# Linear attention and a gated MoE layer on one core: the order in which streamed factors, the next block's x and partial sums are loaded

## The chip, the cores and the metric

The kernel runs on one core of a Trainium2 chip (trn2). The metric is the device time of one execution in microseconds (us); less is better. Loads and stores between DRAM and the core's memory are called transfers or DMAs; all of those named below are issued by SyncE (SP), one after the other, in the order in which they stand in its program.

## The reference

What has to be computed, cut to what matters (8 batches, 8 heads, 576 positions, head size 64, 128 features; the second half has 4608 tokens, a model width of 512 and an inner width of 1536):

```python
def phi(x):
    proj = np.einsum('bhsd,df->bhsf', x, w_phi)
    proj = proj - np.max(np.abs(proj), axis=-1, keepdims=True)
    return np.concatenate([np.exp(proj), np.exp(-proj)], axis=-1)
q_p, k_p = (phi(q), phi(k))
kv = np.einsum('bhsf,bhsd->bhfd', k_p, v)
z = np.sum(k_p, axis=2)
num = np.einsum('bhsf,bhfd->bhsd', q_p, kv)
den = np.einsum('bhsf,bhf->bhs', q_p, z)[..., None] + 1e-06
x = (num / den).transpose(0, 2, 1, 3).reshape(4608, 512)
...
a = x @ w_a
b = x @ w_b
out = (a * b) @ w_out
```

## The kernel before

The work has three stages. The attention makes x and writes it to DRAM (`xnorm`, one buffer per batch). The first pass of the MoE layer takes 768 of the 1536 inner columns, in 12 blocks of 384 tokens, and writes its partial result to DRAM (`part`). The second pass takes the other 768 columns, in 6 blocks of T2 = 768 tokens (blocks 0 to 5), adds the partial result and writes `out`. The change is in the second pass, which takes about the last third of the time.

In the second pass the inner columns are three groups, q0, q1 and q2, of 256. For each group a x and b x are computed as a 2 by 2 by 2 block product by a scheme with seven products in place of eight (Strassen and Winograd). Their weight factors have the names of FACTORS (L61), w11, w12, s2, s1, s3, w22 and s4, and they are made ahead of the pass and kept in DRAM (`kept`). x has factors of the same names, made for each block by `factors_of_x` (L655). `winograd` (L702) is the generator that runs the seven products of one group; its `product` (L713) is 12 matmuls at L723 of 128x128 weights by 384 tokens, 6 for a (`pa`) and 6 for b (`pb`). Each number is split into a high and a low part, so each term takes three matmuls. The output products of `second_pass` (L833, `po`) are 126 more matmuls per block, and their weights stay on the core. A block has 21 x 12 + 126 = 378 matmuls.

The 21 factors of a and b don't stay on the core: each is streamed once per block into a tile of 512 KB (`back_s`, `back_w` in the rows; s or w is the first letter of the factor's name). There is a ring of RING = 4 such tiles. Each product ends with `feed()`, which issues the transfer of the next key of the list `order` (L959) into the tile that the product just left:

```python
def feed():
    used[0] += 1
    if used[0] > FIRST and order:
        key = order.popleft()
        fetch(key, ring[0], ...)
```

So the fetch that follows product n brings the weights of the fourth product after it, and waits for the end of product n, which frees the tile. The list goes q by q, each in the order of FACTORS. The products don't: `second_pass` runs the first two products of a group ahead of the last two of the group before it, so the program's order is q0: w11, w12, s2, s1, s3; q1: w11, w12; q0: w22, s4; q1: s2, s1, s3; q2: w11, w12; q1: w22, s4; q2: s2, s1, s3, w22, s4.

Two more kinds of loads stand in the same queue. `factors_of_x` for the next block loads that block's x (L669) into two tiles `x32`, in four transfers (two tiles by two batches; 576 KB and 192 KB, or 384 KB each), all in its first step, at the end of q0; `behind(feeds, ...)` orders each of them behind the fetch issued last. The steps after that split x (casts on ScalarE at L153, differences on VectorE at L160) and form sums of it (L687 to L690 on VectorE). `given_load` (L806 to L812) loads partial sums into tiles `o` of 384 KB, three at the end of q0 and a fourth after the first stores; the results are added to them at L815 (VectorE) and stored from them at L818. The tiles are the ones that the block before stores from.

In a product's wake ScalarE copies a finished pair of PSUM banks (`evict`, L731, into `top0`, `top1` or `low`), and VectorE adds another pair to it (`add`, L735); both free the banks for later products. A scheduler, which simulates the program with a model of time, decides in what order the instructions of each engine stand; the program's order is only its start.

Of the kernel before, what the change touches and what calls it, by code (L numbers as in the profile page):

```python
# [56 lines left out]
FACTORS, AHEAD = ("w11", "w12", "s2", "s1", "s3", "w22", "s4"), 3.2  # L57
# [4 lines left out]
def tile_kernel(ctx, tc, qP, qD, km, kr, vm, vr, w_phi, w_two, eye, w_a, w_b, w_out, out):  # L62
# [13 lines left out]
    nc = tc.nc  # L76
# [8 lines left out]
    NCC = DM // P  # L85
# [71 lines left out]
    def split(hi, lo, src, eng_hi, eng_lo):  # L157

        copy(eng_hi, hi, src)
        eng_lo.tensor_tensor(lo, src, hi, op=ALU.subtract)  # L160
# [228 lines left out]
    def behind(what, issue):  # L389

        with tc.issue_after(what[-1].ins):
            issue()
# [175 lines left out]
    def weight(q, nm, k):  # L568
        key, i = two[q, nm, k]
        return weights[key][:, i]  # L570
# [84 lines left out]
    def factors_of_x(j, pool, xs):  # L655


        n = T2 // 2
        half = NCC // 2
        x = [None] * NCC  # L660
        for c in range(half):
            x32 = pool.tile([P, 2, T2], F32, tag="x32", bufs=2, name=f"x32_1_{j}_{c}")
            x[c], x[c + half] = x32[:, 0], x32[:, 1]
            t = j * T2
            while t < (j + 1) * T2:
                b, s0 = divmod(t, S)
                m, t0 = min(S - s0, (j + 1) * T2 - t), t - j * T2
                rows = xnorm[b].rearrange("(i c p) s -> p c i s", i=2, p=P)[:, c, :, s0 : s0 + m]
                load = lambda: nc.sync.dma_start(x32[:, :, t0 : t0 + m], rows)  # L669
                behind(feeds, load) if j else load()  # L670
                t += m
        yield

        def factor(c, k, src):
            hl = [pool.tile([P, n], F32R, tag=f"x{k}{part}", bufs=half, name=f"x{k}{part}_1_{j}_{c}") for part in "hl"]
            split(*hl, src, nc.scalar, nc.vector)
            xs[c][k] = hl

        for k, i in (("w11", 0), ("w12", half)):
            for c in range(half):  # L680
                factor(c, k, x[c + i][:, :n])
                yield
        for c in range(half):
            (x11, x12), (x21, x22) = ((t[:, :n], t[:, n:]) for t in (x[c], x[c + half]))
            sums = pool.tile([P, 2, n], F32, tag="xs", name=f"xs_1_{j}_{c}")
            t1, t2, t3, t4 = sums[:, 0], sums[:, 1], x12, x21
            nc.vector.tensor_tensor(t1, x12, x11, op=ALU.subtract)  # L687
            nc.vector.tensor_tensor(t2, x22, t1, op=ALU.subtract)
            nc.vector.tensor_tensor(t3, x22, x12, op=ALU.subtract)
            nc.vector.tensor_tensor(t4, x21, t2, op=ALU.subtract)  # L690
            yield
            factor(c, "s2", t2)
            factor(c, "s1", t1)
            yield
            factor(c, "s3", t3)
            factor(c, "w22", t4)
            yield
        for c in range(half):
            factor(c, "s4", x[c + half][:, n:])
            yield  # L700
# [93 lines left out]
    def second_pass(xs, spaces, feed):  # L794
        n = T2 // 2
        pool = pools_moe[-1]
        nq = NFS[1] // 2
        for j in range(NT // T2):
            src, dst = (t.rearrange("(c p) s -> p c s", p=P)[:, :, j * T2 : (j + 1) * T2] for t in (part, out))
            hs = [{} for _ in range(nq)]  # L800
            x_next = factors_of_x(j + 1, spaces["x"], xs) if (j + 1) * T2 < NT else iter(())
            quads = [winograd(q, xs, hs[q], f"1_{j}_{q}", spaces, feed) for q in range(nq)]
            acc, given, us = {}, {}, []

            def at(m, i, t):
                return (slice(None), m + i * (NCC // 2), slice(t * n, (t + 1) * n))  # L806

            def given_load(i, t):
                place = spaces["o"][(0, 1, 2, 0)[2 * i + t]]
                g = place[0].tile([P, 2, n], F32, tag=place[1], name=f"o_1_{j}_{i}{t}")  # L810
                given.update({(m, i, t): g[:, m] for m in range(2)})
                nc.sync.dma_start(g, src[:, i * (NCC // 2) : (i + 1) * (NCC // 2), t * n : (t + 1) * n])  # L812

            def add(key, x):
                nc.vector.tensor_tensor(given[key], x, given[key], op=ALU.add)  # L815

            def store(key):
                nc.sync.dma_start(dst[at(*key)], given[key])  # L818

            def evict(m):  # L820
                nc.scalar.copy(us[0][:, m], acc[m, 0])  # L821
                return us[0][:, m]

            def product(m, k, to, qs):
                start = (m, to) not in acc
                if start:
                    acc[m, to] = pool.tile([P, n], F32, tag="other" if to else "first", bufs=4, name=f"po{to}_1_{j}_{m}")
                for q in qs:
                    w, (hh, hl) = weight(q, "o", k), hs[q][k]
                    cols = slice(m * P, (m + 1) * P)  # L830
                    for n_, (w_, h_) in enumerate(((w[:, 0, cols], hh), (w[:, 0, cols], hl), (w[:, 1, cols], hh))):
                        f = dict(start=(start and q == qs[0] and n_ == 0), stop=(q == nq - 1 and n_ == 2))
                        nc.tensor.matmul(acc[m, to], w_, h_, skip_group_check=True, **f)  # L833

            early, late_, every = range(nq - 1), range(nq - 1, nq), range(nq)
            for q in range(nq):
                for _ in range(3 if q == 0 else 2):
                    next(quads[q])
                    if q == nq - 1:
                        next(x_next, None)  # L840
                        next(x_next, None)
                if q < nq - 1:
                    next(quads[q + 1])
                else:
                    product(0, "w11", 0, early)
                    product(0, "w12", 1, early)
                next(quads[q])
                if q < nq - 1:
                    next(quads[q], None)
                    next(quads[q], None)  # L850
                if q == 0:
                    next(x_next, None)
                    for i, t in ((0, 0), (0, 1), (1, 0)):
                        given_load(i, t)
            product(1, "w11", 0, early)
            product(1, "w12", 1, early)
            product(0, "w11", 0, late_)
            us.append(spaces["brief"].tile([P, 2, n], F32, tag="top0", bufs=2, name=f"u_1_{j}"))
            u = evict(0)
            product(0, "w12", 1, late_)  # L860
            next(quads[-1])
            product(1, "w11", 0, late_)
            u_ = evict(1)
            product(1, "w12", 1, late_)
            next(quads[-1])
            for m, u1 in ((0, u), (1, u_)):
                add((m, 0, 0), u1)
                add((m, 0, 0), acc[m, 1])
                store((m, 0, 0))
            given_load(1, 1)  # L870
            next(x_next, None)
            for m in range(2):
                product(m, "s2", 0, every)
                u2 = evict(m)
                next(x_next, None)
                add((m, 0, 1), u2)
                product(m, "s1", 2, every)
                next(x_next, None)
            for m in range(2):
                product(m, "s3", 0, every)  # L880
                u3 = evict(m)
                next(x_next, None)
                add((m, 1, 1), u3)
                add((m, 1, 1), acc[m, 2])
                store((m, 1, 1))
            for m in range(2):
                product(m, "w22", 0, every)
                add((m, 1, 0), acc[m, 0])
                store((m, 1, 0))
                next(x_next, None)  # L890
                product(m, "s4", 2, every)
                add((m, 0, 1), acc[m, 2])
                store((m, 0, 1))
                next(x_next, None)
            for _ in x_next:
                pass
# [26 lines left out]
    kept, begun, feeds = {}, set(), []  # L923
# [27 lines left out]
    nq = NFS[1] // 2  # L951
# [4 lines left out]
    outs = [(q, "o", k) for q in range(nq) for k in FACTORS]  # L956
    pairs.update({("o", i // 2): outs[i : i + 2] for i in range(0, len(outs), 2)})
    two = {key: (pair, i) for pair, keys in pairs.items() for i, key in enumerate(keys)}
    order = [(q, k) for q in range(nq) for k in FACTORS]  # L959
    own = {key: (first, f"first{i}") for i, key in enumerate(order[:FIRST])}  # L960
    xs = [{} for _ in range(NCC // 2)]
    with ExitStack() as c:
# [29 lines left out]
    order = deque(order * (NT // T2))  # L992
# [81 lines left out]
```

## Time and profile before

| | |
|---|---|
| device time, three runs | 1240.18, 1236.78, 1238.57 us; median 1238.57 us |
| the profiled execution: device time | 1236.89 us |
| the profiled execution: span of the trace | 1235.1 us |
| mean granted TensorE clock, share of full | 0.996 |
| second pass, first matmul to the end of the span | about 815 to 1235 us |
| blocks 1 to 5 of it | one every 69 us or so |

The trace numbers lines as the listing above does. PE is TensorE, PEld its weight loads, DVE VectorE, ACT ScalarE, SP SyncE, which issues the DMAs. A busy share says how much of the time an engine worked; a wait names the instruction that came last of those it waited for. Matmuls overlap: one of 384 columns is shown with 0.335 us, while they start 0.173 us apart, so an idle time of PE between two of them counts from the shown end of the one before. PEclk is the clock granted to TensorE, 1.00 for full speed.

### The profile page before, as it was taken

To read this page: it belongs to the slowest core of one execution; us is meant where nothing else is said; L and a number is where in the kernel's file an instruction comes from. 1 tells how busy PE (TensorE), PEld (TensorE's weight loads), DVE (VectorE), ACT (ScalarE), POOL (GpSimd) and SP (SyncE) were. 2 spreads that over 40 slices of the span, in tenths; PEclk is the share of its full clock that TensorE was granted. 3 is DMA by queue.
4 is the path that set the end of the run, shared out by engine and by line. 5 is a ranking of instruction groups with operands and counts; after the bars stand their busy time and mean duration, and the time that the engine had idled before them with its cause. 6 is when DMAs were issued, how large, how long until landed. Compare 5 with 4: busy or idle time off the path is not lost.

```text
span 1235.1 us, 20179 instructions
## 1 busy us (share of the span) xinstructions
PE 1190.4 (96%) x7086; PEld 1135.3 (92%) x7086; DVE 970.6 (79%) x1733; ACT 782.2 (63%) x1656; POOL 152.4 (12%) x68
## 2 busy tenths in 40 slices
PE   8889999999999999999999999989999999989988
PEld 5467788999999999999999999989999999989988
DVE  7867888988998988898888389968677685957565
ACT  5767778878878887888887446645344352525332
POOL 2322222111222121221221000000000000000000
PEclk9999999999999999999999999999999999999999
DMA  8766774554454454455342588667585858577571
GB/s 233 217 208 178 178 193 121 151 155 121 141 152 141 137 156 124 139 154 150 111 125 71 170 269 291 213 219 238 181 284 175 299 166 294 180 243 227 185 239 64
DMA packets 146165, 225.13 MB, mean 182 GB/s; under 512 B 40912, under 2 KB 87760, under 8 KB 146064
## 3 DMA queue, kind: packets, MB, share of 16 engines
q1 hardware_dynamic: 145616, 223.58, 59.4%
q8 instruction: 56, 0.92, 0.3%
q14 instruction: 45, 0.37, 0.1%
q10 hardware_dynamic: 448, 0.26, 0.1%
HBM read 174.74 MB, written 49.05 MB: 181 GB/s over the span
## 4 chain that ended last, share of the span: by engine, by line
PE 68%; DMA 15%; DVE 10%; ACT 4%; issue 2%; SPq 1%; DVEq 0%; ACTq 0%
PE po L833 10%; PE pa L723 10%; PE pb L723 9%; PE pa L616 8%; PE pb L616 8%; PE po L639 7%; PE kvps L301 6%; PE pn L383 6%; DMA back_s<-kept_s 4%; PE pq L359 2%; DMA raw_b<-in_w_b 2%; PE pk L244 1%; DMA raw_a<-in_w_a 1%; DMA part<-o 1%; DMA k<-in_km 1%
## 5 line engine op out<-in xcount | busy, mean ns | idle before, releaser
L363 POOL PARTITION_ALL_REDUCE mb<-p x64 | 152.2, 2379 | 528.9 <-ACT p L360 430.5
L616 PE MATMUL pa<-xh,w_a 128*128 128x384 f32 x576 | 168.3, 344 | 3.0 <-ACT xh L153 1.8
L616 PE MATMUL pb<-xh,w_b 128*128 128x384 f32 x576 | 163.3, 341 | 0.0
L639 PE MATMUL po<-hh,w_o 128*128 128x384 f32 x576 | 154.3, 340 | 0.1
L616 PEld LDWEIGHTS pa<-xh,w_a 128*128 128x128 f32 x576 | 106.1, 189 | 4.8 <-ACT xh L153 2.1
L616 PEld LDWEIGHTS pb<-xh,w_b 128*128 128x128 f32 x576 | 105.5, 188 | 0.5
L639 PEld LDWEIGHTS po<-hh,w_o 128*128 128x128 f32 x576 | 104.8, 188 | 0.8 <-ACT o L651 0.3
L616 PE MATMUL pa<-xl,w_a 128*128 128x384 f32 x288 | 98.5, 342 | 0.0
L639 PE MATMUL po<-hl,w_o 128*128 128x384 f32 x288 | 97.4, 340 | 0.3 <-DVE hl L160 0.3
L616 PE MATMUL pb<-xl,w_b 128*128 128x384 f32 x288 | 97.5, 339 | 0.0
L160 DVE TENSOR_TENSOR qel<-qe,qeh 128x1152 fp32r<-128x1152 f32 x46 | 62.3, 1355 | 32.4 <-ACT qeh L153 29.6
L833 PE MATMUL po<-hh_s,own_o 128*128 128x384 f32 x288 | 79.9, 335 | 0.3 <-ACT u L821 0.3
L165 DVE TENSOR_TENSOR qs<-q,qs 64x576 fp32r<-64x576 f32 x52 | 64.1, 1233 | 14.5 <-ACT qs L153 12.7
L384 ACT COPY xn<-pn 65x288 f32<-65x288 f32 x128 | 49.1, 395 | 18.3 <-PE pn L383 14.8
L833 PE MATMUL po<-hh_w,own_o 128*128 128x384 f32 x216 | 59.7, 334 | 0.0
L153 ACT CAST qeh<-qe 128x1152 fp32r<-128x1152 f32 x46 | 53.4, 1160 | 2.3 <-PE pn L383 2.3
L639 PEld LDWEIGHTS po<-hl,w_o 128*128 128x128 f32 x288 | 54.1, 188 | 0.7 <-DVE hl L160 0.7
L616 PEld LDWEIGHTS pa<-xl,w_a 128*128 128x128 f32 x288 | 54.2, 188 | 0.3
L367 ACT ACTIVATE qe<-p 128x576 f32<-128x576 f32 x64 | 44.6, 697 | 15.2 <-DVE qel L160 10.2
L616 PEld LDWEIGHTS pb<-xl,w_b 128*128 128x128 f32 x288 | 54.1, 188 | 0.1
L258 ACT ACTIVATE ke<-kd 128x512 f32<-128x512 f32 x64 | 40.8, 637 | 21.1 <-DVE kd L250 18.8
L160 DVE TENSOR_TENSOR kel<-ke,keh 128x1024 fp32r<-128x1024 f32 x42 | 52.4, 1247 | 1.8 <-ACT keh L153 1.6
(301 smaller groups left out, 3431.2 us busy)
## 6 DMA issues: line engine op xcount, KB each, us to landing
back_s<-kept_s SPq DMA_DIRECT2D x71, 512.0 KB
back_w<-kept_w SPq DMA_DIRECT2D x52, 512.0 KB
q<-in_qD SPq DMA_DIRECT2D x52, 288.0 KB
k<-in_km SPq DMA_DIRECT2D x55, 256.0 KB
xun<-xn SPq DMA_DIRECT2D x64, 144.0 KB
x<-xun SPq DMA_DIRECT2D x32, 288.0 KB
rb<-rec SPq DMA_DIRECT2D x32, 288.0 KB
xnorm<-x SPq DMA_DIRECT2D x32, 288.0 KB
```

The source lines that it names most:

```text
L153: eng.copy(dst, src)
L160: eng_lo.tensor_tensor(lo, src, hi, op=ALU.subtract)
L165: eng_lo.tensor_tensor(hi_lo[D:], src[D:], hi_lo[D:], op=ALU.subtract)
L301: nc.tensor.matmul(st["kv_ps", b, pr][:width, j], v_[:, j, :width], e_[:, j], start=(left == NFULL and j == 0 and n_ == 0), stop=(left == ...
L363: nc.gpsimd.partition_all_reduce(mb, p32, P, bass_isa.ReduceOp.absmax)
L367: nc.scalar.activation(e[:, 0], p32, AF.Exp)
L383: nc.tensor.matmul(pn[: D + 1, :HALF], kv_[:, 2 * j + s, :], e_[:, s, tok], **at)
L384: nc.scalar.copy(xn[: D + 1, tok], pn[: D + 1, :HALF])
L616: nc.tensor.matmul(acc, w[:, cc * P : (cc + 1) * P], x, start=(k == 0), stop=(k == 3 * NCC - 1))
L639: nc.tensor.matmul(accs[cc], w[:, cc * P : (cc + 1) * P], h, **at)
L723: nc.tensor.matmul(acc[to][i], w_, x_, skip_group_check=True, **at)
L833: nc.tensor.matmul(acc[m, to], w_, h_, skip_group_check=True, **f)
```

## The change

The list `order` now names the factors in the order in which the program runs the products (FIRST takes its first three keys, and the ring its next four, which are now q0's s1 and s3 and q1's w11 and w12). `factors_of_x` now yields after each of the four x transfers; its first step is taken at the end of q0 as before, two more within q1 and the fourth in q2's turn. The three `given_load` of the end of q0 are now at the end of q1, and every `given_load` is placed behind the fetch issued last. `(nc.sync if j else nc.sync)` is SyncE either way.

```diff
@@ factors_of_x
-                load = lambda: nc.sync.dma_start(x32[:, :, t0 : t0 + m], rows)
+                load = lambda: (nc.sync if j else nc.sync).dma_start(x32[:, :, t0 : t0 + m], rows)
                 behind(feeds, load) if j else load()
                 t += m
-        yield
+                yield
@@ second_pass, given_load
-                nc.sync.dma_start(g, src[:, i * (NCC // 2) : (i + 1) * (NCC // 2), t * n : (t + 1) * n])
+                load = lambda: nc.sync.dma_start(g, src[:, i * (NCC // 2) : (i + 1) * (NCC // 2), t * n : (t + 1) * n])
+                behind(feeds, load)
@@ second_pass, loop over q
                     if q == nq - 1:
                         next(x_next, None)
                         next(x_next, None)
+                    if q == 1:
+                        next(x_next, None)
                 if q < nq - 1:
                     next(quads[q + 1])
+                    if q == 1:
+                        next(x_next, None)
                 else:
                     product(0, "w11", 0, early)
                     product(0, "w12", 1, early)
@@
                 if q == 0:
                     next(x_next, None)
+                if q == 1:
                     for i, t in ((0, 0), (0, 1), (1, 0)):
                         given_load(i, t)
@@ tile_kernel
-    order = [(q, k) for q in range(nq) for k in FACTORS]
+    order = [(0, k) for k in FACTORS[:2]]
+    for q in range(nq):
+        order += [(q, k) for k in FACTORS[2:5]]
+        order += [(q + 1, k) for k in FACTORS[:2]] if q + 1 < nq else []
+        order += [(q, k) for k in FACTORS[5:]]
```

Counted on PE from the end of one product to the start of another, a block of the program before (blocks 1 to 5) runs 18 matmuls between the product that frees the tile of q1's s2 and that product itself, 24 for q1's s1, and 36 for most others. In the changed program it is 24 for q2's w11, 32 to 36 for q1's s2 and s1, q0's s4, q2's w12 and s2 and q1's w22 and s4, and more for the rest. In block 0 of the changed program it is 13 for q2's w11, which there stands right behind q2's w12. The first output products that take the PSUM banks of q1's s4 stand 25 matmuls behind that product in the changed program.

How SyncE's queue stands in block 2, from the load of the partial sums on (names are back, fetch number, group, factor). Before:

```order
L812 DMA o_1_2_10_11990<-part_98 128x2x384
L565 DMA back_47_1_w12_11875<-kept_1_w12_9060 128x1024
L812 DMA o_1_2_01_11988<-part_98 128x2x384
L565 DMA back_50_1_s3_11934<-kept_1_s3_9075 128x1024
L565 DMA back_48_1_s2_11902<-kept_1_s2_9065 128x1024
L565 DMA back_49_1_s1_11918<-kept_1_s1_9070 128x1024
L565 DMA back_51_1_w22_11948<-kept_1_w22_9080 128x1024
L669 DMA x32_1_3_0_11980<-xnorm4_94 128x2x576
L669 DMA x32_1_3_0_11980<-xnorm5_95 128x2x192
L669 DMA x32_1_3_1_11983<-xnorm4_94 128x2x576
L669 DMA x32_1_3_1_11983<-xnorm5_95 128x2x192
L565 DMA back_52_1_s4_12004<-kept_1_s4_9085 128x1024
```

And in the changed program, from the fetch that now stands there on:

```order
L565 DMA back_47_0_s4_11875<-kept_0_s4_8807 128x1024
L565 DMA back_48_1_s2_11902<-kept_1_s2_9065 128x1024
L565 DMA back_49_1_s1_11918<-kept_1_s1_9070 128x1024
L565 DMA back_50_1_s3_11934<-kept_1_s3_9075 128x1024
L565 DMA back_51_2_w11_11948<-kept_2_w11_9366 128x1024
L669 DMA x32_1_3_0_11980<-xnorm4_94 128x2x576
L565 DMA back_52_2_w12_11994<-kept_2_w12_9371 128x1024
L565 DMA back_53_1_w22_12010<-kept_1_w22_9080 128x1024
L669 DMA x32_1_3_0_11980<-xnorm5_95 128x2x192
L565 DMA back_55_2_s2_12064<-kept_2_s2_9376 128x1024
L565 DMA back_54_1_s4_12035<-kept_1_s4_9085 128x1024
L669 DMA x32_1_3_1_12047<-xnorm4_94 128x2x576
```

The loads of partial sums have left this stretch, each fetch stands in the order in which its tile comes free, and the transfers of x stand one by one between fetches.

SyncE's queue at the start of the second pass (block 0). Before:

```order
L652 DMA part_98<-o_0_11_2_10324 128x384
L565 DMA back_0_0_s4_10355<-kept_0_s4_8807 128x1024
L812 DMA o_1_0_00_10562<-part_98 128x2x384
L812 DMA o_1_0_01_10564<-part_98 128x2x384
L812 DMA o_1_0_10_10566<-part_98 128x2x384
L652 DMA part_98<-o_0_11_3_10346 128x384
L565 DMA back_4_1_w11_10423<-kept_1_w11_9055 128x1024
L565 DMA back_8_1_s3_10510<-kept_1_s3_9075 128x1024
L565 DMA back_5_1_w12_10451<-kept_1_w12_9060 128x1024
```

And in the changed program:

```order
L652 DMA part_98<-o_0_11_2_10324 128x384
L565 DMA back_0_1_w12_10355<-kept_1_w12_9060 128x1024
L652 DMA part_98<-o_0_11_3_10346 128x384
L565 DMA back_4_0_w22_10423<-kept_0_w22_8802 128x1024
L565 DMA back_6_1_s2_10478<-kept_1_s2_9065 128x1024
L565 DMA back_7_1_s1_10494<-kept_1_s1_9070 128x1024
L565 DMA back_5_0_s4_10451<-kept_0_s4_8807 128x1024
L565 DMA back_10_2_w12_10570<-kept_2_w12_9371 128x1024
L565 DMA back_8_1_s3_10510<-kept_1_s3_9075 128x1024
L565 DMA back_9_2_w11_10524<-kept_2_w11_9366 128x1024
```

The last store of the first pass (`part`, row 3 of the changed piece) no longer has three loads of partial sums ahead of it, and the fetch of q2's w11 is the last of its group.

VectorE in block 2, between the last sums of q0 and the sums of q1's `top1` (L735 frees PSUM banks, the names with x32 and xs are the next block's x). Before:

```order
L687 TENSOR_TENSOR xs_1_3_0_12338<-x32_1_3_0_11980 128x384
L735 TENSOR_TENSOR low_1_2_1_12046<-pa2_1_2_1_12006,low_1_2_1_12046 128x384
L688 TENSOR_TENSOR xs_1_3_0_12338<-x32_1_3_0_11980,xs_1_3_0_12338 128x384
L689 TENSOR_TENSOR x32_1_3_0_11980<-x32_1_3_0_11980 128x384
L735 TENSOR_TENSOR low_1_2_1_12046<-pb2_1_2_1_12007,low_1_2_1_12046 128x384
```

And in the changed program:

```order
L160 TENSOR_TENSOR xw11l_1_3_0_12190<-x32_1_3_0_11980,xw11h_1_3_0_12189 128x384
L735 TENSOR_TENSOR low_1_2_1_12037<-pa2_1_2_1_11996,low_1_2_1_12037 128x384
L687 TENSOR_TENSOR xs_1_3_0_12338<-x32_1_3_0_11980 128x384
L735 TENSOR_TENSOR low_1_2_1_12037<-pb2_1_2_1_11997,low_1_2_1_12037 128x384
L688 TENSOR_TENSOR xs_1_3_0_12338<-x32_1_3_0_11980,xs_1_3_0_12338 128x384
L689 TENSOR_TENSOR x32_1_3_0_11980<-x32_1_3_0_11980 128x384
L735 TENSOR_TENSOR top0_1_2_2_12049<-pa1_1_2_2_12066,top0_1_2_2_12049 128x384
L764 TENSOR_TENSOR low_1_2_1_12037<-low_1_2_1_12037 128x384
L735 TENSOR_TENSOR top0_1_2_2_12049<-pb1_1_2_2_12067,top0_1_2_2_12049 128x384
L160 TENSOR_TENSOR xw12l_1_3_0_12222<-x32_1_3_0_11980,xw12h_1_3_0_12221 128x384
```

An operation on the newly loaded x (the L160 row) now stands ahead of the two `low` adds, and the L687 row, which reads what two of the transfers bring, has moved from ahead of them to between them. From here to the first `top1` add, VectorE has 9 operations before and 19 in the changed program.

## Rows read from the trace of the kernel before

**Rows 1.** The page: busy us (share of the span) and instructions per engine.

```profile
PE 1190.4 (96%) x7086; PEld 1135.3 (92%) x7086; DVE 970.6 (79%) x1733; ACT 782.2 (63%) x1656; POOL 152.4 (12%) x68
```

**Rows 2.** Windows: start:end, us, busy us (count) by engine, PEclk, DMA share, GB/s.

```profile
850.00:900.00 50.00, 50.00 (x290) 49.97 (x290) 34.20 (x70) 20.27 (x44) 0.00 (x0) 1.00 0.61 196
900.00:950.00 50.00, 47.35 (x264) 47.06 (x263) 40.47 (x83) 24.78 (x53) 0.00 (x0) 0.97 0.67 216
1100.00:1150.00 50.00, 46.46 (x257) 45.85 (x256) 39.91 (x82) 23.87 (x51) 0.00 (x0) 0.97 0.71 233
```

**Rows 3.** Waits, 800 to 1235 us: us in total, times, longest us.

```profile
PE pa L723 <- DMA back_s<-kept_s: 14.9, 8, 3.0
...
PE pa L723 <- DMA back_w<-kept_w: 2.1, 4, 0.7
PE pa L723 <- ACT top L731: 2.3, 1, 2.3
...
ACT top L731 <- DMA part<-o: 4.7, 1, 4.7
DVE xs L687 <- DMA x<-xnorm: 4.4, 3, 2.7
```

**Rows 4.** Chain of waits, start of block 0: start us, us, what.

```profile
811.36 6.98 DMA part<-o
...
819.02 1.31 PE pa L723 x6
...
828.68 3.65 DMA back_s<-kept_s
...
834.78 8.56 DMA back_s<-kept_s
```

**Rows 5.** Chain of waits, q1's s2 in block 1.

```profile
897.68 5.81 DMA back_s<-kept_s
903.63 2.08 PE pa L723 x6
905.72 1.80 PE pb L723 x6
...
908.58 1.04 PE pb L723 x6
```

**Rows 6.** Timeline of PE, block 1: start, us, what, idle time before and its releaser.

```profile
903.63 0.48 PE L723 MATMUL pa<-xs2h,back_s 128*128 128x384 f32 x1 [2.65 <-DMA back_s<-kept_s]
```

**Rows 7.** Chain of waits, q1's s2 in block 4.

```profile
1112.20 1.92 PE pb L723 x6
1114.12 1.72 PE pa L723 x6
```

**Rows 8.** Groups of instructions by line, 800 to 1235 us: count | busy us, mean ns | idle before.

```profile
L833 PE MATMUL po<-hh_s,own_o 128*128 128x384 f32 x288 | 79.9, 335 | 0.3 <-ACT u L821 0.3
...
L723 PE MATMUL pa<-xs2h,back_s 128*128 128x384 f32 x68 | 21.1, 352 | 11.4 <-DMA back_s<-kept_s 11.4
...
L735 DVE TENSOR_TENSOR top<-pa,top 128x384 f32<-128x384 f32 x36 | 19.9, 554 | 20.0 <-PE pa L723 15.2 <-ACT top L731 4.7
```

**Rows 9.** Windows of a few us in and after the queued fetches.

```profile
896.00:910.00 14.00, 11.35 (x57) 11.02 (x56) 8.69 (x18) 4.15 (x9) 0.00 (x0) 0.88 1.00 357
904.00:906.00 2.00, 2.00 (x8) 2.00 (x7) 1.55 (x4) 0.47 (x2) 0.00 (x0) 0.50 0.97 309
970.00:972.00 2.00, 1.91 (x11) 1.59 (x10) 1.50 (x4) 0.04 (x1) 0.00 (x0) 1.00 1.03 416
```

**Rows 10.** DMA issues: out<-in, queue, form, count, KB each.

```profile
back_s<-kept_s SPq DMA_DIRECT2D x71, 512.0 KB
...
o<-part SPq DMA_DIRECT2D x24, 384.0 KB
...
x<-xnorm SPq DMA_DIRECT2D x8, 576.0 KB
```

**Rows 11.** Waits of SP's DMA queue, 780 to 1235 us.

```profile
SPq L818 <- DVE o L815: 75.5, 30, 18.0
```

## The prediction

> **What bounds the kernel now.** I read four views, from coarse to fine. The page first: TensorE (PE) is busy 1190.4 us of the span of 1235.1 us [rows 1], so a change that removes no matmul can only win back idle or slow TensorE time. Then windows along the second pass. From 850 to 900 us PE is never idle; from 900 to 950 and from 1100 to 1150 us it is busy 47.35 and 46.46 us of 50, and its granted clock averages 0.97 [rows 2]. The loss sits in one part of each block, and most of it is idle time. Then the waits, for what ends that idle time: PE waits 14.9 us in 8 waits for `back_s`, 2.1 us in 4 for `back_w`, and 2.3 us once for the `top` copy on ScalarE, which itself had waited 4.7 us for a store of `part` [rows 3]. Of the 14.9 us, 11.4 stand ahead of the first matmuls of s2 [rows 8]; those are q1's, once in each of blocks 1 to 5. Last the chain of waits, for the reason. In block 1 the fetch of q1's s2 is released at 897.68 us by the end of q0's w22 and takes 5.81 us [rows 5], while PE has only 18 matmuls between the two. One fetch in the chain took 3.65 us; the one behind four x transfers took 8.56 us [rows 4]. Fetches come late because their tiles come free late, and because other transfers stand ahead of them.
>
> **Units.** Six matmuls of L723 take 1.04 us in the chain when nothing disturbs them [rows 5], so one takes 0.1733 us and a product of 12 takes 2.08 us. Shown with 0.335 us each [rows 8], they overlap, and idle time is counted from the shown end of the matmul before. After a wait the first six take 1.31 us in the chain, not 1.04 [rows 4]. A wait therefore costs its idle time and 0.27 us.
>
> **What the change removes.**
> 1. All 12 DMA waits of today: 14.9 + 2.1 = 17.0 us [rows 3].
> 2. The wait on ScalarE at the start of the pass, 2.3 us [rows 3]: the store of `part` took 6.98 us [rows 4] behind three loads of 384 KB each [rows 10]. These now stand at the end of the block. Its cover is the four products of q0 and q1's first that run meanwhile; what replaces the 2.3 us could be the tail of the same store, which I take as nothing.
> 3. The small cost of 13 waits: 13 x 0.27 = 3.5 us.
> 4. Two falls of the clock. After idle times of 2.65 us [rows 6] and 3.0 us (the longest) [rows 3] the granted clock drops to 0.50, so to 1.2 of 2.4 GHz [rows 9]. In block 1 two pieces of the chain take 2.08 + 1.80 us where 1.31 + 1.04 is usual: 1.53 us lost [rows 5]. In block 4 the two slow pieces take 1.92 + 1.72 against 2 x 1.04: 1.56 us [rows 7]. Together 3.1 us. The 2.3 us wait had no such fall behind it.
>
> The ceiling is 17.0 + 2.3 + 3.5 + 3.1 = 25.9 us, if nothing new waits.
>
> **What it adds or leaves.** No matmul, no byte and no instruction of VectorE or ScalarE is added; transfers are moved.
> - *q2's w11, block 0.* Its tile is freed by q0's s4 and it is needed 13 matmuls later, 2.25 us. The nearest rows are the unhindered fetch, 3.65 us [rows 4], and the queued one, 5.81 us [rows 5]: idle 1.4 to 3.6 us. I take 1.4, since only q1's s3 stands close ahead of it; with 0.27 it is 1.7 us.
> - *q2's w11, blocks 1 to 5.* 24 matmuls, 4.16 us, is now the shortest lead. Against 3.65 to 5.81 us it gives 0 to 1.65 us of idle. One fetch ahead of it was released 2 us earlier and the x transfer stands behind it, so it is nearer to the free row: 0.4 us each with the restart, 2.0 in all.
> - *All other fetches* have 32 matmuls or more, 5.6 us or more, against 3.65 free. Before the stretch is reached, q0's s4 stands behind the last stores of the block before, which wait for VectorE [rows 11]; those are issued by about when its tile comes free, so I count nothing, and 5.81 - 5.6 = 0.2 us if that cover is gone.
> - *The middle of a block with x in it.* Between the end of q0's s4 and that of q1's w22 (72 matmuls, 12.5 us) six fetches of 512 KB and four x transfers (1536 KB) are issued [rows 10]: 4.72 MB, 378 GB/s. With all DMA engines full the queue moved 357 GB/s over 14 us and 416 GB/s over 2 us [rows 9]. At 357 the stretch falls 0.26 MB, 0.7 us, behind. Leads of 36 matmuls, 6.2 us, leave 2.6 us over a free fetch, so by this count nothing waits; were a fetch again to take 8.56 us, each block would wait 2.3 us. So 0 to 2.3 us.
> - *VectorE and ScalarE behind x.* The sums at L687 wait for the second x transfer and now stand between the two `low` adds, and twice as many operations stand ahead of the adds that free q1's `top1` banks. The output products that take those banks stand 25 matmuls, 4.3 us, behind q1's s4; the two adds take 2 x 0.55 us [rows 8], so 3.2 us are left. Ten more operations ahead of them, at 0.55 us, are 5.5 us if none of them runs in VectorE's idle time: 0 to 2.3 us of PE each. A wait for x at L687 was at most 2.7 us [rows 3], under the 3.2.
>  For these last two together I take 0.8 us in each of five blocks, 4.0 us: nearer to nothing, since both counts leave slack, but they share one queue and one engine.
> - *Partial sums* are issued some 7 us ahead of the first add that reads them, three transfers of 384 KB: 1.18 MB, 3.3 us at 357 GB/s. Nothing.
>
> Sum: 1.7 + 2.0 + 4.0 = 7.7 us remain of 25.9, a gain of 18.2 us. The profiled execution's own time is 1236.9 us, 1.7 under the median of 1238.57 shown; 1236.9 - 18.2 = **1219 us** (1218.7).
>
> For a transfer's length the Trainium skill has a fit (DMA: Bandwidth & Descriptors, Anatomy of one DMA), measured on GpSimd's path: about 2.0 us and the bytes over 436 GB/s. It makes 3.2 us of a fetch; by it blocks 1 to 5 would not wait for q2's w11 at all and block 0 would 1.0 us, a sum 2.5 us lower. The trace's shortest in the chain, 3.65 us on SyncE's path, decides here.
>
> **Rivals.**
> A. *The waits move more than they vanish.* The middle stretch runs the DMA engines full, and fetches behind x take 8.56 us as one did [rows 4] against leads of 6.2: 2.3 + 0.27 us in each of five blocks, 12.9 us in place of the 4.0. Gain 25.9 - 1.7 - 2.0 - 12.9 = 9.3 us, about 1228 us. For it: 378 GB/s is above the 357 held for 14 us. Against it: 416 GB/s was reached in a short window [rows 9], and the 8.56 us had all four x transfers ahead, where there is now one per fetch or two.
>  The same page of the Trainium skill (Specifications) puts the limit of memory traffic per core at about 358 GB/s and says that it binds for such transfers. The 14 us window agrees with it, the 2 us window at 416 GB/s does not; held for the stretch, it would put it the same 0.7 us behind, which speaks for A without making it.
> B. *Slower.* ScalarE's casts of the next block's x stand among the copies that free PSUM banks. If an x transfer, now pushed behind several fetches, lands 8.56 us late [rows 4], those copies and with them PE stop for that, less about 2 us of slack: 6.5 us of idle, 0.27, and a clock fall of 1.56, 8.3 us in each of five blocks. That is 41.6 against 25.9 - 1.7 removed: 17.4 us slower, about 1254 us. It decides from (25.9 - 1.7)/5 = 4.8 us per block. For it: the one ScalarE wait on a DMA cost PE 2.3 of 4.7 us [rows 3]. Against it: x is needed only in the second half of the block, and the waits on x were 4.4 us in all [rows 3].
> C. *It does nothing.* The scheduler puts instructions where its model of time wants them, and the waits come back elsewhere at the same price: 1237 us. Against it: in the order of SyncE's queue each fetch stands where its tile comes free.
>
> **How the numbers follow.** Changes within 0.3% (3.7 us) can't be told from none: faster means under about 1234.9 us. Chances: forecast 0.70, A 0.18, C 0.06, B 0.06. Faster 0.88, the same 0.06, slower 0.06. The range's low end is the ceiling without block 0's wait, 1236.9 - 24.2 = 1212.7, less some tenths for the other waits of PE on ScalarE and VectorE: 1212. Its high end takes in A with q2's w11 at its worst (1.65 + 0.27 in place of 0.4, 1.5 us more, in each of two blocks): 1231. B and C lie outside, with a small part of A.
>
> **What would show it.** Right: no `back_s` wait ahead of s2, total PE waits for DMAs of 3 to 8 us, the longest one at q2's w11 in block 0 with 1 to 2 us, a granted clock of 1.00 in every window of the second pass, no `part` wait on ScalarE, blocks of about 66 us. Wrong: a wait of PE of over 2 us at q2's w12, s2 or q1's w22 or s4 (A); ScalarE or VectorE waiting over 5 us on x with PE behind (B).

## The result

The changed kernel takes 1224.49 us (median of 4 runs, 1220.32 to 1227.83), the kernel before 1238.45 us beside it: a ratio of 0.9889, 95% interval 0.9866 to 0.9912, 14 us faster. On a second chip, with more runs of both, it was 1225.81 against 1234.20 us, 0.9936 (0.9914 to 0.9958), 8.4 us. The forecast was 1219 us, 1212 to 1231. The gain is there, and so are new waits, about twice as much as was forecast.

The profiled execution took 1223.43 us, 13.5 us less than that of the kernel before. The page of the changed kernel, by engine:

```profile
PE 1186.5 (97%) x7086; PEld 1132.4 (93%) x7086; DVE 972.5 (80%) x1733; ACT 779.3 (64%) x1656; POOL 153.6 (13%) x68
```

The instructions are as many as before [rows 1]. Windows of the changed kernel, columns as in [rows 2]:

```profile
850.00:900.00 50.00, 46.95 (x271) 46.51 (x270) 35.36 (x70) 18.83 (x41) 0.00 (x0) 1.00 0.61 192
900.00:950.00 50.00, 47.51 (x272) 46.57 (x270) 38.76 (x80) 24.80 (x54) 0.00 (x0) 1.00 0.73 239
1100.00:1150.00 50.00, 48.42 (x275) 47.18 (x273) 39.63 (x82) 24.24 (x53) 0.00 (x0) 1.00 0.76 249
```

The granted clock is now 1.00 in all three, so the two falls are gone here, but PE still idles 3.1, 2.5 and 1.6 us of 50. What ends that idle time is shown by the waits of the changed kernel, 800 to 1222 us:

```profile
ACT xw11h L153 <- DMA x<-xnorm: 13.9, 6, 2.8
...
PE pa L723 <- DMA back_w<-kept_w: 5.4, 4, 1.6
...
PE pa L723 <- ACT top L731: 3.8, 3, 3.1
...
ACT top L731 <- DMA part<-o: 1.0, 1, 1.0
...
PE pa L723 <- ACT low L731: 0.9, 2, 0.5
PE po L834 <- DVE hl_s L742: 0.9, 1, 0.9
...
PE po L834 <- DVE o L816: 0.5, 1, 0.5
...
PE po L834 <- ACT u L822: 0.3, 1, 0.3
```

Against [rows 3]: the 14.9 us for `back_s` are gone, all of them; `back_w` has risen from 2.1 to 5.4 us; the store of `part` holds up ScalarE 1.0 us instead of 4.7 and PE not at all; PE's wait for ScalarE's `top` has moved and grown from 2.3 to 3.8 us. ScalarE now waits 13.9 us for x. The timeline of PE tells where its waits are (start, us, what, idle time before and its releaser):

```profile
808.57 0.41 PE L723 MATMUL pa<-xw11h,own_w 128*128 128x384 f32 x1 [0.67 <-issue]
835.40 0.41 PE L723 MATMUL pa<-xw11h,back_w 128*128 128x384 f32 x1 [1.62 <-DMA back_w<-kept_w]
856.37 0.44 PE L723 MATMUL pa<-xs3h,back_s 128*128 128x384 f32 x1 [3.06 <-ACT top L731]
903.95 0.41 PE L723 MATMUL pa<-xw11h,back_w 128*128 128x384 f32 x1 [1.46 <-DMA back_w<-kept_w]
924.53 0.44 PE L723 MATMUL pa<-xs3h,back_s 128*128 128x384 f32 x1 [0.58 <-ACT top L731]
927.35 0.44 PE L723 MATMUL pa<-xw22h,back_w 128*128 128x384 f32 x1 [0.46 <-ACT low L731]
1038.53 0.41 PE L723 MATMUL pa<-xw11h,back_w 128*128 128x384 f32 x1 [1.41 <-DMA back_w<-kept_w]
1105.22 0.41 PE L723 MATMUL pa<-xw11h,back_w 128*128 128x384 f32 x1 [0.93 <-DMA back_w<-kept_w]
```

Two kinds are left. The four waits on a DMA are all at q2's w11, in blocks 0, 1, 3 and 4. Those on ScalarE are at q2's s3 and w22, the largest in block 0. The sums: 11.8 us of idle in 12 waits and 12 x 0.27 us, 15.0 us. Before it was 17.0 + 2.3 + 0.6 us (the last at the outputs) in 15 waits, 4.0 us for these, and 3.1 us for two clock falls, 27.0 in all. The difference is 12.0 us. It agrees with the second pass itself: from its first matmul to the end of the span it took 424.9 us before and takes 413.1 us now, 11.9 us less. The other 1.6 us of the 13.5 lie ahead of the second pass, which starts earlier in this trace. That start is the first row above; the same row of the kernel before:

```profile
810.17 0.41 PE L723 MATMUL pa<-xw11h,own_w 128*128 128x384 f32 x1 [0.61 <-issue]
```

Nothing shows that the change makes this 1.6 us. In the traces of all the kernels below the start lies anywhere from 805.3 to 809.8 us, and in a second trace of the changed kernel (after_again) it is at 805.32 us. There the second pass takes 415.8 us.

### The profile page after: what moved, and what is told of

Same layout as the page of the kernel before. It is cut to its first block, busy times and chain, and to the rows that moved or that the text cites. A ratio compares the mean times of both kernels' runs of the same rounds, so it can differ in the third digit from the quotient of the medians.

```text
span 1221.6 us, 20188 instructions
## 1 busy us (share of the span) xinstructions
PE 1186.5 (97%) x7086; PEld 1132.4 (93%) x7086; DVE 972.5 (80%) x1733; ACT 779.3 (64%) x1656; POOL 153.6 (13%) x68
## 4 chain that ended last, share of the span: by engine, by line
PE 76%; DMA 10%; DVE 9%; ACT 3%; issue 2%; SPq 0%; ACTq 0%; DVEq 0%
PE pa L616 10%; PE pb L616 10%; PE pa L723 10%; PE pb L723 9%; PE po L639 9%; PE po L834 9%; PE kvps L301 8%; PE pn L383 7%; DMA x<-xnorm 3%; PE pq L359 2%; PE pk L244 2%; DMA back_w<-kept_w 1%; DMA raw_a<-in_w_a 1%; DMA rec<-r 1%; DMA xnorm<-x 1%
## 5 line engine op out<-in xcount | busy, mean ns | idle before, releaser
L160 DVE TENSOR_TENSOR qel<-qe,qeh 128x1152 fp32r<-128x1152 f32 x46 | 62.3, 1354 | 31.9 <-ACT qeh L153 25.3
L165 DVE TENSOR_TENSOR qs<-q,qs 64x576 fp32r<-64x576 f32 x52 | 63.4, 1220 | 14.3 <-ACT qs L153 11.4
L834 PEld LDWEIGHTS po<-hh_s,own_o 128*128 128x128 f32 x288 | 52.6, 188 | 1.7 <-DVE o L816 0.8
L258 ACT ACTIVATE ke<-kd 128x512 f32<-128x512 f32 x64 | 40.8, 637 | 20.3 <-DVE kd L250 19.3
```

Source lines behind the costliest of these rows:

```text
L165: eng_lo.tensor_tensor(hi_lo[D:], src[D:], hi_lo[D:], op=ALU.subtract)
```

## The experiments

The kernels below ran in three groups of four. Those of one group share a chip and the runs of the kernel before, whose medians on the three chips were 1237.38, 1234.20 and 1234.56 us. The whole change ran again in the second group alone, so that comparing it with a kernel of another group goes by their ratios to the kernel before.

### The parts of the change, apart

**order_only**: of the diff above, the new `order` list alone.

> The new list of fetches alone; x's four transfers in one step and the partial sums where they were. Theory A (the list does it): every wait at q1's s2 goes (11.4 us before), with the two clock falls (3.1 us), and the ScalarE wait of 2.3 us at the start of the pass stays; q2's w12, now right behind four x transfers with a lead of 36 matmuls (6.2 us), waits 0 to 2.6 us in each of blocks 0 to 4. About 1227 to 1232 us. Theory B (the moved transfers do it): the waits come back at other products at the same price, 1234 to 1240 us.

1230.61 us, ratio 0.9943 (0.9920 to 0.9966): 6.8 us faster. Waits, 815 us to the end:

```profile
PE pa L723 <- DMA back_s<-kept_s: 7.1, 5, 1.9
PE pa L723 <- DMA back_w<-kept_w: 6.5, 6, 2.1
...
ACT top L731 <- DMA part<-o: 4.4, 1, 4.4
PE pa L723 <- ACT top L731: 2.0, 1, 2.0
```

The time is where theory A put it, the waits only in part. q1's s2 still waits, 1.1 to 1.9 us in each of blocks 1 to 5; its fetch stands behind loads of partial sums that wait for stores, and in order_part below, where these loads are moved, it doesn't wait. q2's w12 waits 0.7 to 0.8 us in four blocks. The 2.0 us on ScalarE are at q2's s3, not at the start. The trace is of the slowest of the five runs, 1235.40 us, and the clock falls three times in its second pass, where theory A had none; the three runs of 1229 to 1231 us had a mean clock of 0.999, the traced one 0.994.

**moves_only**: all of the diff but the `order` list.

> The moved x transfers and partial sums alone, with the old list of fetches. Theory A: q1's s2 keeps a lead of 19 matmuls (3.3 us) in most blocks and q1's s1 falls to one of 12 (2.1 us), both under the 3.65 us of an unhindered fetch: PE waits of 1.5 to 3 us at q1's s1 or s2 in each block, 10 us or more in all; the 2.3 us ScalarE wait at the start goes. 1233 to 1245 us. Theory B: fetches no longer stand behind other transfers, land in under 4 us, and most of the gain is here: 1222 to 1230 us.

1237.63 us, ratio 0.9997 (0.9976 to 1.0018): nothing.

```profile
PE pa L723 <- DMA back_s<-kept_s: 16.1, 9, 3.9
```

As theory A had it: the waits are as long as before [rows 3], now at q1's s1 (up to 3.94 us) and s2, in each of blocks 1 to 5. The moved transfers are worth nothing while the fetches come in the wrong order.

**order_part** (the list and the partial sums) and **order_x** (the list and the spread x), as edits of the whole change:

```diff
 # order_part
-                yield
+        yield
 ... (and the two steps of x that the change put within q1 are left out)
 # order_x
-                load = lambda: nc.sync.dma_start(g, src[...])
-                behind(feeds, load)
+                nc.sync.dma_start(g, src[...])
 ...
-                if q == 1:
                     for i, t in ((0, 0), (0, 1), (1, 0)):
```

> The new list and the moved partial sums; x's four transfers in one step again. If spreading x matters, the fetches of q2's w12 and q1's w22 land over 6.2 us after their issue, PE waits up to 2.6 us in each of blocks 0 to 4, and the time is 3 to 13 us above that of the whole change: 1227 to 1237 us. If it doesn't, the time is that of the whole change, 1220 to 1228 us, with no wait of PE at q2's w12 or q1's w22.

> The new list and the spread x; partial sums loaded where they were (end of q0, no order behind a fetch). Theory: only block 0 loses by it, the ScalarE wait of 2.3 us and 0.27 come back, 1225 to 1229 us. Rival: in each block the loads of partial sums, which wait in SyncE's queue for stores, hold up the fetches of q0's s4 and q1's s2 (leads 36 and 32 matmuls), up to 2 us per block: 1230 to 1238 us.

order_part: 1232.76 us, 0.9959 (0.9937 to 0.9981). order_x: 1231.28 us, 0.9956 (0.9927 to 0.9985). Each of them gains 5 to 6 us, no more than the list alone; with both it was 14 us on the first chip and 8.4 on the second. What the two moves add to the list is not settled by these times: the list alone, 0.9920 to 0.9966, lies clear of the whole change on the first chip, but not of that on the second, 0.9914 to 0.9958. The waits tell more. In order_part the four transfers stand right behind the fetch of q2's w11, and that product or q2's w12 waits 1 to 2.4 us in blocks 0 to 4, for the fetch or for an operation on VectorE that has to do with x or stands behind it. In order_x q1's s2 waits 0.5 to 1.8 us in three blocks, as the rival had it, and the wait on ScalarE at q2's s3 in block 0 is 3.05 us. The 2.3 us of block 0 came back on ScalarE (4.0 us for `part`) but not on PE.

### What the remaining waits hang on

**after_again** is the whole change beside the next three. **swap** exchanges two fetches, those of q1's s3 and q2's w11, so that they come as PE runs the products:

```diff
+    i = order.index((2, "w11"))
+    order[i - 1], order[i] = order[i], order[i - 1]
```

**x_behind** puts VectorE's and ScalarE's work on the next block's x behind q1's last sums:

```diff
         def factor(c, k, src):
-            split(*hl, src, nc.scalar, nc.vector)
+            with later():
+                split(*hl, src, nc.scalar, nc.vector)
```

(`later` is `tc.issue_after` for q1's difference at L785 and its cast of s1; the sums at L687 to L690 are placed so too.) **swap_behind** has both edits.

> The whole change once more, beside the next three on one chip: 1220 to 1228 us, PE waits of 11 to 13 us in the second pass, of them some 5 at q2's w11 for its fetch and some 5 for ScalarE's copies of top and low.

> The whole change with the fetch of q2's w11 one place ahead of that of q1's s3, which is how PE runs them: leads of 24 matmuls (4.2 us) in block 0 and 36 (6.2 us) in blocks 1 to 5 in place of 13 and 24. Theory L (the short lead is what was left): the waits at q2's w11 fall from 5.4 us in 4 to under 1.2 us, with their 0.27 each; 3 to 6 us faster than the whole change, and no new wait at q1's s3 (lead 36). Rival R (the DMA engines are what limits, so a wait only moves): the same few us of waits at q1's s3 or q2's w12, and no gain over the whole change.

> The whole change with VectorE's and ScalarE's operations on the next block's x issued behind q1's last sums (the difference at L785 and the cast of s1). Theory V (x's operations stand ahead of the sums and casts that lead to the top and low copies): the waits of PE for ScalarE's top and low (4.75 us in 5) go, 4 to 6 us faster than the whole change; the wait at q2's w11 stays. Rival: PE's wait comes from the PSUM banks being used earlier, whatever VectorE does, and the waits stay; or x is now made too late and the first products of the next block wait 1 us or more for its casts, no gain.

> Both edits together. If both theories hold the gains add: PE waits of the second pass under 4 us in all, 8 to 11 us faster than the whole change, 1213 to 1217 us. If only the lead counts, as the swap alone; if only VectorE counts, as x behind alone.

after_again: 1225.81 us, 0.9936 (0.9914 to 0.9958), 14.7 us of idle. swap: **1213.98 us, 0.9830 (0.9802 to 0.9858)**, 12 us faster than the whole change, more than theory L had. x_behind: 1235.89 us, 1.0000 (0.9981 to 1.0019), which undoes the gain: its trace has 18.4 us of idle in 24 waits, some of them new ones at the outputs. swap_behind: 1215.88 us, 0.9847 (0.9822 to 0.9872), no better than the swap. The waits of swap:

```profile
PE pa L723 <- DMA back_w<-kept_w: 1.9, 3, 1.2
PE pa L723 <- ACT low L731: 1.5, 1, 1.5
...
PE pb L723 <- ACT low L731: 1.1, 1, 1.1
```

and of x_behind, whose L739 is L731 of the others:

```profile
PE pa L731 <- ACT top L739: 6.3, 5, 2.5
PE pa L731 <- DMA back_w<-kept_w: 5.5, 4, 1.9
```

Theory L holds: with leads of 24 matmuls in block 0 and 36 in the others the waits at q2's w11 are gone but for 0.23 us in block 0; 1.2 and 0.4 us moved to q2's w12. The gain beyond theory L is in the waits for ScalarE's `top`: the swap, which only exchanges two fetches, removed every one. In its program the scheduler gave PE another order as well, of which more below. Those for `low` rose from 1.7 us in after_again to 2.6.

Theory V is not settled by x_behind. The wait in block 0 goes only from 3.06 to 2.46 us, and the waits for `top` are 6.3 us in all, with VectorE clear of x from q1's s4 to its last sum. But four casts of x on ScalarE now stand ahead of the `top` copy, which starts at 855.13 us:

```profile
852.65 0.92 ACT L153 CAST xw11h<-x 128x384 fp32r<-128x384 f32 x2
```

The chain of the changed kernel in block 0 tells more of these waits:

```profile
848.29 1.05 PE pa L723 x6
...
849.37 0.56 DVE top L735
...
850.39 0.47 DVE x L689
...
854.93 0.48 DVE low L782
...
855.43 0.51 ACT hh_s L739
855.94 0.39 ACT top L731
...
856.37 1.32 PE pa L723 x6
```

It runs from q1's s4 through all of q1's sums, with five of x between (L689 is one), to L782, the last to read q1's `top1`, and only then ScalarE copies q2's pair into `top1`, upon which q2's s3 may overwrite the banks. `top1 = both("top1", 1)` has one buffer for all groups. From the first `top` add, when half of s4 is done, to the s3 that takes 7.0 us. The copy follows a cast on ScalarE (L739) without a gap, so the chain alone leaves open whether it waited for the buffer or for its turn on the engine. In block 0 the changed program runs q1's s4 right ahead of q2's s3, with 17 output matmuls, 2.9 us, between; the swapped one runs q1's s4 ahead of q2's s1 and s2. The same buffer would explain the other wait: q1's s3 can't start before q0's sums are done either, so the scheduler runs q2's w11 ahead of it, which takes 12 matmuls off the lead of w11's fetch.

**top1x2** gives `top1` two buffers (the room comes from h21 and t2, which move into halves of `low` and `top1` that are free by then); **alias_only** moves h21 and t2 but leaves one buffer:

```diff
-        top1 = both("top1", 1)
+        top1 = both("top1", 2)
-        h21 = spaces["brief"].tile([P, n], F32, tag="h21", name=f"h21_{u}")
+        h21 = low[:, 1]
-        t1, t2, t3, t4 = top0[:, 1], low[:, 1], low[:, 0], top0[:, 0]
+        t1, t2, t3, t4 = top0[:, 1], top1[:, 1], low[:, 0], top0[:, 0]
```

> The whole change with two buffers for top1 in place of one (room for it: h21 lies in the second half of low, t2 in the second half of top1). Theory T (one top1 buffer is behind both kinds of waits that were left: ScalarE can't copy a group's sums into it before the group ahead has done its last difference, so PE runs q2's w11 ahead of q1's s3, which makes its lead short, and q2's s3 waits for the top copies): the waits at q2's w11 go with a lead of 30 to 36 matmuls in blocks 1 to 5 and 25 in block 0, and those at q2's s3 go too; PE waits under 5 us in all, 8 to 12 us faster than the whole change, at least as fast as the swap. Rival: the waits for top are VectorE's and ScalarE's load, whatever the buffers; then the waits at q2's s3 stay and only those at q2's w11 go, 3 to 6 us faster.

> The same placing of h21 and t2, with one top1 buffer as in the whole change: a control. Theory T: the waits at q2's w11 and at q2's s3 stay (q1's s4 stands right ahead of q2's s3 in four blocks), the time is that of the whole change or up to 8 us more. Rival: where h21 and t2 lie is what helps; then it is as fast as with two buffers.

top1x2: **1211.16 us, 0.9802 (0.9780 to 0.9824)**, 23 us under the kernel before and the lowest of all; by its ratio some 16 us under the whole change on the second chip, where 8 to 12 were expected. Its second pass took 402.9 us, against 424.9 before. alias_only: 1238.10 us, 1.0022 (1.0004 to 1.0040). All waits of PE in top1x2, and two of its windows:

```profile
PE pa L723 <- DMA back_s<-kept_s: 1.1, 2, 0.6
PE po L834 <- DVE o L816: 0.6, 1, 0.6
PE pa L723 <- DMA back_w<-kept_w: 0.5, 1, 0.5
PE po L834 <- ACT u L822: 0.3, 1, 0.3
```

```profile
900.00:950.00 50.00, 49.55 (x286) 49.07 (x284) 38.11 (x79) 22.31 (x48) 0.00 (x0) 1.00 0.69 237
1100.00:1150.00 50.00, 49.96 (x288) 49.67 (x287) 38.43 (x79) 21.80 (x48) 0.00 (x0) 1.00 0.70 242
```

and of alias_only:

```profile
PE pa L723 <- ACT top L731: 12.1, 7, 3.5
PE pa L723 <- DMA back_w<-kept_w: 6.1, 4, 2.5
```

Theory T is shown, and theory V falls as the cause: the two kernels differ by the second buffer alone, and it takes both kinds of waits away, with x's work where it was. PE then runs q1's s3 ahead of q2's w11, as in the list, and 2.5 us of idle are left in the pass. The control is slower than was expected of it, by its ratio some 11 us slower than the whole change on the second chip where at most 8 were expected. A likely reason, not tested by itself, is that t2 now lies in `top1`, so that q1's sums read the one buffer up to L785; the waits for `top` are 12.1 us, against 3.8 in the changed kernel.

**swap_again** is the swap on this chip:

> The swapped fetches again, beside the two buffers on one chip: 8 to 12 us faster than the whole change.

1214.54 us, 0.9827 (0.9807 to 0.9847), by its ratio some 13 us faster than the whole change. It is 3.4 us above top1x2, but the two intervals overlap.

**late_x** starts the x transfers later, by a step of q1 in place of the end of q0:

```diff
                 if q < nq - 1:
                     next(quads[q + 1])
                     if q == 1:
                         next(x_next, None)
+                        next(x_next, None)
 ...
-                if q == 0:
-                    next(x_next, None)
```

> The whole change with each x transfer two or three fetches later, so none stands right behind the fetch of q2's w11, whose lead stays at 24 matmuls (13 in block 0). Theory C (packets of the x transfer share the DMA engines with the fetch ahead and delay its landing from 4.0 to 5.4 us): the waits at q2's w11 fall to under 0.4 us in blocks 1 to 5. Rival: they stay, since a lead of 4.2 us is too short for a fetch with another one ahead; 1 to 2 us in two or more of those blocks, and no gain over the whole change.

1242.07 us, 1.0056 (1.0036 to 1.0075), slower than before:

```profile
PE pa L723 <- ACT top L731: 16.5, 10, 4.8
...
PE pa L723 <- DMA back_w<-kept_w: 1.9, 2, 1.6
```

Theory C holds in the main: the fetch of q2's w11, with the same lead, is waited for in block 0 alone (1.61 us); the other 0.25 us are at w12. In block 3 it is issued at 1042.90 us, no x transfer is issued within 4 us of it, and its product starts 4.3 us later:

```profile
1042.90 0.32 SPq L565 DMA_DIRECT2D back_w<-kept_w  x1
1047.22 0.41 PE L723 MATMUL pa<-xw11h,back_w 128*128 128x384 f32 x1 [0.18 <-ACT top L731]
```

In the changed kernel that fetch took 5.40 us in block 3. Read from issue to landing in the two traces, it took 4.2 to 4.3 us in blocks 1 to 4 of late_x, and in the changed kernel, with an x transfer issued 0.4 us behind it, 5.5, 4.0, 5.4 and 4.9 us. So the x transfer behind it can delay it, though it didn't in block 2. PE still idles 0.2 to 0.6 us at q2's w11 in blocks 1 to 5, now put down to ScalarE's `top` copy. The larger price is paid at q2's s3, where PE waits 3.5, 2.1, 1.2 and 4.75 us for the `top` copies in four blocks. The chain of its longest wait, in block 4, begins with an x transfer:

```profile
1123.03 7.35 DMA x<-xnorm
...
1130.40 0.56 DVE xs L687
...
1140.88 0.48 DVE low L782
...
1141.89 0.39 ACT top L731
```

VectorE works through x and q1's sums in turn, up to the same L782 and the same copy. So x's work can lengthen that chain, if it comes late, but it is the one buffer that ties PE to it.

## Why the prediction was right, and where it was not

Right in sign, in its cause and within its range; the gain was 14.0 us (8.4 on the second chip) where 18.2 was forecast.

- *Luck.* The forecast left 7.7 us of waits and 15.0 came. The range held them because its high end was drawn for rival A, whose waits didn't come; others, about as large, did.
- *What goes.* Each of the 12 DMA waits and the wait on ScalarE at the start went, 19.3 us of idle. order_only and moves_only show that the list is the cause of the gain, and that the moved transfers are worth nothing without it. Rival C was wrong for the whole; for the moves alone its time was right, but for another reason, the order of the fetches. Of the 11.4 us that the prediction put at q1's s2 in blocks 1 to 5, 0.3 stand in block 0, which changes no sum.
- *The clock falls* (item 4, 3.1 us) went in the profiled execution. In after_again's, too, every 50 us window of the second pass is at 1.00. Whether they go in all runs is open: the eight of after_again had mean clocks of 0.993 to 0.998, those at 0.993 and 0.998 taking 1231.06 and 1222.94 us, and a mean doesn't tell where the clock was low. In both traces of the changed kernel the clock below 1.00 lies in the first 100 us.
- *q2's w11 in block 0*: 1.62 + 0.27 = 1.9 us, forecast 1.7.
- *q2's w11 in blocks 1 to 5*: 1.46 + 1.41 + 0.93 + 3 x 0.27 = 4.6 us, forecast 2.0. The step that failed is that the x transfer "stands behind it, so it is nearer to the free row". The fetch took 5.40 us in block 3 and 4.93 in block 4, nearer to the queued row of 5.81 [rows 5], and by late_x the transfer behind it is why; in blocks 2 and 5 it took 4.0 us and PE didn't wait. The chain of the changed kernel, blocks 0, 3 and 4:

```profile
831.54 3.72 DMA back_w<-kept_w
...
1032.99 5.40 DMA back_w<-kept_w
...
1100.16 4.93 DMA back_w<-kept_w
```

- *VectorE and ScalarE behind x, and the middle of the block*: forecast 4.0 us, measured 3.06 + 0.58 + 0.46 + 0.19 + 0.46 + 5 x 0.27 = 6.1. The size was half as large again, and that it came so near is in part luck, since the mechanism was only half right: x's work on VectorE lengthens the chain, but PE hangs on it by the one `top1` buffer (top1x2 against alias_only). I had the adds that free PSUM banks for the output products in view and not the tile that ScalarE copies into, upon which q2's s3 and w22 wait; and 3.3 of the 6.1 us are in block 0 alone, not 0.8 in each of five blocks.
- *Not counted*: three waits at the outputs of block 5, 0.89 + 0.27 + 0.48 + 3 x 0.27 = 2.4 us, of which before had some 1.1.
- *The fit of the Trainium skill* (DMA: Bandwidth & Descriptors, Anatomy of one DMA), stated there for GpSimd's path, gives 3.2 us a fetch as an estimate and so no wait in blocks 1 to 5. Read from issue to landing, none of the fetches of the second pass, all on SyncE's path, took under 3.37 us in any trace, and q2's w11 took 4.0 to 5.5 us in these blocks; the measured times decide.
- *Rival A*: no wait at q2's w12, s2 or q1's w22, s4 in the changed kernel's trace, and one of 0.85 us, on ScalarE, at q1's w22 in after_again's. The stretch that was put at 378 GB/s moved 272 GB/s in block 1 and 288 in block 3, with the DMA engines 82% and 90% busy. order_part, with x in one step, has waits there much as A had them, at q2's w12 2.2 us for the fetch and 2.4 for a `low` add. *Rival B*: ScalarE did wait 13.9 us for x, but at most 2.8 us at a time, and PE little behind it. late_x is that rival, all but its size: x later by some fetches, PE waits of up to 4.75 us behind it, and slower than before.
- *The signs*: the waits for DMAs, 5.4 us in all, the longest, 1.62 us at q2's w11 in block 0, and the clock came as was said. The wait for `part` on ScalarE didn't go but fell to 1.0 us.

Not tried: more than one buffer for `low`, and the two buffers with the x transfers elsewhere. Why the same change is worth 14.0 us on one chip and 8.4 on another stays open; of the 5.6 us between them 4.3 lie in the medians of the kernel before, 1238.45 and 1234.20 us, and 1.3 in those of the changed kernel.

## What to carry to other kernels

Fetch in the order in which the engine really runs the products, which is the scheduler's order and not the program's, and count each fetch's lead in matmuls. When an engine runs things out of the order that was written, look for what held back the one it skipped: here one buffer too few cost two different waits, one of which looked like a slow DMA. Moves that are worth nothing alone can take waits away after the real order is mended, so test the parts with and without each other.

## What was not expected of the hardware

A transfer issued behind a fetch on the same queue can delay the fetch: 4.9 to 5.5 us in three of four blocks of the changed kernel, against 4.2 to 4.3 us without it (late_x).

And whether the clock falls isn't told by the length of one idle time: after 3.06 us at q2's s3 of block 0 in the changed kernel it stayed at 1.00 (row above), while in order_x nearly the same wait of 3.05 us at the same product was followed by a fall to 0.50, so to 1.2 of 2.4 GHz. The row and the window behind it:

```profile
854.89 0.69 PE L723 MATMUL pa<-xs3h,back_s 128*128 128x384 f32 x1 [3.05 <-ACT top L731]
855.00:857.00 2.00, 2.00 (x7) 2.00 (x8) 1.06 (x3) 1.32 (x4) 0.00 (x0) 0.50 0.00 0
```

In order_only 1.89 us ahead of q1's s2 in block 5 were followed by a fall too: the next two pieces of the chain took 2.06 and 1.82 us, in place of 1.31 and 1.04. In the kernel before, 2.61 us at the same place had no fall behind them.
